# Cached GQA decode block: P·V two steps behind its scores, K three transfers ahead of V, and a last batch that gives o^T by head group

## The chip, the cores and the metric

The kernel runs on one core of a Trainium2 chip. The metric is the device time of one execution in microseconds (us); lower is better. Engines are called as the profile calls them: PE is TensorE (PEld are its weight loads), DVE is VectorE, ACT is ScalarE, POOL is GpSimd and SP is SyncE, which here issues nearly all DMAs. Sixteen DMA engines move the data of all DMAs of the core.

## The reference

A block of grouped-query attention with a cached K and V: 32 batches of 4 query rows each, 32 query heads, 4 K/V heads (a group of 8 query heads shares one), 2048 cached positions, head width 128, everything in bf16.

```python
B, Sq, D = 32, 4, 1024
Hq, Hkv, Sk, Dh = 32, 4, 2048, 128
q = (x @ wq).reshape(B, Sq, Hq, Dh).transpose(0, 2, 1, 3)
k = jnp.repeat(k_cache, rep, axis=1)          # k_cache, v_cache: [B, Hkv, Sk, Dh]
v = jnp.repeat(v_cache, rep, axis=1)
scores = jnp.einsum("bhqd,bhkd->bhqk", q, k) * (Dh ** -0.5)
p = softmax(scores, axis=-1)
o = jnp.einsum("bhqk,bhkd->bhqd", p, v)
return o.transpose(0, 2, 1, 3).reshape(B, Sq, Hq * Dh) @ wo
```

K and V of one batch are 2 MB each, so 128 MB of the cache have to be read once, and wq and wo are 8 MB each.

## The kernel before, in words

Every operation is put on the list of its engine by `p.op` or `p.dma` (lines 26 and 33), with the names of the operations that it waits for. Each engine runs its list strictly in the order written; a wait is a semaphore wait ahead of the instruction. So the order of the Python code is the order on each engine, and what is queued behind a waiting instruction waits too.

**Start.** x and wq are loaded, `Q^T` of all batches is made (line 176) and copied to `QT_sb` (lines 187, 189).

**One batch, called a step.** The loop at line 320 runs over the 32 batches. 128 rows of the score tile are 4 K/V groups by 32 (8 heads by 4 queries). Step i does, in this order on PE:

- `pe_qk(i)`, line 240: 16 matmuls give the scores of batch i in `ps_s`, 128x2048, four PSUM banks. `softmax_max` on DVE reads them (line 280), `softmax_exp` on ACT makes `P_sb` (line 285), `softmax_rinv` on DVE the reciprocal of the row sums (line 290).
- `pe_ot(i-2)`, line 271: one transpose of `o_sb` of batch i-2; ACT copies it to `oT_sb` (line 275). After each eighth batch `oproj` (line 296) multiplies the eight batches by wo: 128 matmuls.
- `pe_fill(i+1, f)` for f = 0 to 7, line 207: K of the *next* batch is transposed, eight 128x128 tiles per fill, and copied to `KT_sb` by DVE (f = 2, 3, 5, 7, line 217) or ACT (line 219).
- `pe_pv(i-1)`, line 248: 64 matmuls P·V of the batch one step behind; ACT scales the result by the reciprocal into `o_sb` (line 265).
- `pe_pt(i, f)` for f = 0, 1, line 225: P of batch i is transposed, and DVE copies it to `PT_sb` (line 231). There is one `PT_sb`, so that copy waits for `pe_pv(i-1)`.

All small PSUM tiles come from a ring of four banks (`slot`, line 194): a new tile waits until the tile four before it has been copied out.

**Loads.** SP issues K and V transfers of 2 MB. `K_sb` and `V_sb` have three buffers each. K of batch b waits for the last fill of batch b-3; V of batch b waits for `pe_pv(b-3)`. The order of the loads is written out: K0, K1, then for each b K(b+2), V(b); wo comes in four parts after V2 to V5. The last V, batch 31, comes in four parts of 512 KB, one for each group, each with its own semaphore.

```python
152        load_k(0)
153        load_k(1)
154        for b in range(B):
155            if b + 2 < B:
156                load_k(b + 2)
157            load_v(b)
158            if b in (2, 3, 4, 5):
159                load_wo(b - 2)
```

**End.** After the loop, from line 346: o^T of batch 30; then P·V of batch 31 for groups 0 to 2 and then for group 3 (lines 351 to 356); ACT scales 96 rows and then 32 rows (lines 357, 359); PE transposes them (363, 371) and DVE copies them to `oT_sb` (364, 372); 96 matmuls with wo for the first 24 heads (line 368), 32 for the last 8 (line 374), in a part of `ps_s`; DVE copies the result to `y_sb` (line 309) and the last four output DMAs are issued by SP and ACT (line 313).

Of the kernel before, what the change touches and what calls it, by code (L numbers as in the profile page):

```python
# [5 lines left out]
ACT = mybir.ActivationFunctionType  # L6
ALU = mybir.AluOpType
AX = mybir.AxisListType
BF16 = mybir.dt.bfloat16
# [47 lines left out]
def bass_standalone__gqa_block_cached__sampling_kernel(  # L57
# [8 lines left out]
    B, Sq, D = x.shape  # L66
    _, G, Sk, Dh = k_cache.shape
# [8 lines left out]
    TV = T // C  # L76
    KT = D // 128
    NKB = 3
    NVB = 3
# [3 lines left out]
    OG = 8  # L83
    NOG = B // OG
    NC = D // 4
    scale = float(Dh) ** -0.5
# [5 lines left out]
    with ExitStack() as es:  # L92
        def sbuf(name, shape, dtype):
            return es.enter_context(nc.sbuf_tensor(name, shape, dtype))

        w_sb = sbuf("w_sb", [128, KT, Hq * Dh], BF16)
        wo_sb = w_sb[:, :, :].rearrange("p a (c n) -> p (a c) n", n=D)
        K_sb = sbuf("K_sb", [128, NKB, T, Dh], BF16)
        V_sb = sbuf("V_sb", [128, NVB, G, TV, Dh], BF16)
# [1 line left out]
        QT_sb = sbuf("QT_sb", [128, B, Hq, Sq], BF16)  # L101
        oT_sb = sbuf("oT_sb", [128, Hq, NT], BF16)
        P_sb = sbuf("P_sb", [128, Sk], BF16)
        PT_sb = sbuf("PT_sb", [128, TV, 128], BF16)
        x_sb = P_sb[:, 0:D]
        xT_sb = P_sb[:, D:2 * D].rearrange("p (a b) -> p a b", b=128)
        o_sb = sbuf("o_sb", [128, Dh], BF16)
# [15 lines left out]
        p = _Program()  # L123
# [8 lines left out]
        def load_k(b):  # L132
            p.dma("sp", lambda e: e.dma_start(
                K_sb[:, b % NKB, :, :], k_cache[b].rearrange("g (r t) d -> (g r) t d", r=R)),
                [("fill", b - NKB, NFILL - 1)] if b >= NKB else [], ("k", b), f"s_k{b % NKB}")
# [13 lines left out]
                wo_sb[:, 8 * c:8 * c + 8, :], wo[c * 1024:(c + 1) * 1024, :].rearrange("(h p) n -> p h n", p=128)),  # L149
                ["qproj"], ("wo", c), f"s_w{c}")  # L150

        load_k(0)
        load_k(1)
        for b in range(B):
            if b + 2 < B:
                load_k(b + 2)
            load_v(b)
            if b in (2, 3, 4, 5):
                load_wo(b - 2)
# [34 lines left out]
        def slot(free):  # L194
            n = len(freed)
            freed.append(free)
            return ring[n % NRING], [freed[n - NRING]]
# [13 lines left out]
        def evac(b, f):  # L211
            buf = slot_of["kt", b, f]
            waits = [("fill", b, f)] + ([("qk", b - 1)] if b else [])
            dst = KT_sb[:, f * TB // C:(f + 1) * TB // C, :, :].rearrange("p v g (r c) -> p (v g) r c", c=C)
            src = buf.rearrange("p (c m r) -> p m r c", c=C, r=R)
            if f in DVE_FILLS:
                p.op("dve", lambda e: e.tensor_copy(dst, src), waits, ("kt", b, f))  # L217
            else:
                p.op("act", lambda e: e.activation(dst, src, ACT.Copy), waits, ("kt", b, f))  # L219

        def pe_pt(i, f):
            buf, waits = slot(("pt", i, f))
            buf = slot_of["pt", i, f] = buf.bitcast(BF16)
            for q in range(8):
                p.op("pe", lambda e, q=q: e.transpose(  # L225
                    buf[:, q * 128:(q + 1) * 128], P_sb[:, (8 * f + q) * 128:(8 * f + q + 1) * 128], ident[:, :]),
                    waits + [("exp", i)] if q == 0 else [], ("ptf", i, f) if q == 7 else None)

        def evac_pt(i, f):
            buf = slot_of["pt", i, f]  # L230
            p.op("dve", lambda e: e.tensor_copy(PT_sb[:, 8 * f:8 * f + 8, :].rearrange("p t q -> p (t q)"), buf),  # L231
                 [("ptf", i, f)] + ([("pv", i - 1)] if i else []), ("pt", i, f))


        def pe_qk(i):
# [11 lines left out]
        def pv_mm(buf, i, g, t, waits, done):  # L247
            p.op("pe", lambda e: e.matmul(  # L248
                buf[32 * g:32 * (g + 1), 0:Dh],
                lhsT=PT_sb[:, t, 32 * g:32 * (g + 1)],  # L250
                rhs=V_sb[:, i % NVB, g, t, :],
                start=(t == 0), stop=(t == TV - 1), tile_position=(0, 32 * g)), waits, done)

        def pe_pv(i):
            buf, waits = slot(("o", i))
            slot_of["o", i] = buf
            waits = waits + [("pt", i, 0), ("pt", i, 1), ("v", i)]
            for t in range(TV):
                for g in range(G):
                    pv_mm(buf, i, g, t, waits if t == 0 and g == 0 else [],  # L260
                          ("pv", i) if (t, g) == (TV - 1, G - 1) else None)

        def o_evac(i):
            buf = slot_of["o", i]
            p.op("act", lambda e: e.activation(o_sb[:, :], buf[:, 0:Dh], ACT.Copy, scale=rinv[:, i:i + 1]),  # L265
                 [("pv", i), ("rinv", i)] + ([("oT", i - 1)] if i else []), ("o", i))

        def pe_ot(i):
            buf, waits = slot(("ot", i))
            buf = slot_of["ot", i] = buf.bitcast(BF16)  # L270
            p.op("pe", lambda e: e.transpose(buf[:, 0:128], o_sb[:, :], ident[:, :]), waits + [("o", i)], ("oT", i))  # L271

        def ot_evac(i):
            buf = slot_of["ot", i]
            p.op("act", lambda e: e.activation(  # L275
                oT_sb[:, :, i * Sq:(i + 1) * Sq], buf[:, 0:128].rearrange("p (h s) -> p h s", s=Sq), ACT.Copy),
                [("oT", i)], ("ot", i))
# [15 lines left out]
        def oproj_mm(buf, n, heads, waits, done):  # L293
            for h in heads:
                for j in range(4):
                    p.op("pe", lambda e, h=h, j=j: e.matmul(  # L296
                        buf[32 * j:32 * (j + 1), 0:NC],
                        lhsT=oT_sb[:, h, 32 * n:32 * (n + 1)],
                        rhs=wo_sb[:, h, NC * j:NC * (j + 1)],
                        start=(h == 0), stop=(h == Hq - 1), tile_position=(0, 32 * j)),  # L300
                        waits if (h, j) == (heads[0], 0) else [], done if (h, j) == (heads[-1], 3) else None)
# [15 lines left out]
        for f in range(NFILL):  # L317
            pe_fill(0, f)
            evac(0, f)
        for i in range(B):  # L320
            pe_qk(i)
            softmax_max(i)
            if i >= 2:
                pe_ot(i - 2)
                ot_evac(i - 2)
                if i % OG == 1 and i > 1:
                    oproj(i // OG - 1)
            if i + 1 < B:
                for f in (0, 1):
                    pe_fill(i + 1, f)  # L330
                    evac(i + 1, f)
            softmax_exp(i)
            if i + 1 < B:
                for f in range(2, NFILL):
                    pe_fill(i + 1, f)
                    evac(i + 1, f)
            softmax_rinv(i)
            if i >= 1:
                pe_pv(i - 1)
                o_evac(i - 1)  # L340
            for f in range(2):
                pe_pt(i, f)
                evac_pt(i, f)


        L = B - 1
        pe_ot(L - 1)
        ot_evac(L - 1)
        o_l, waits = slot(None)
        waits = waits + [("pt", L, 0), ("pt", L, 1)]  # L350
        for t in range(TV):
            for g in range(3):
                pv_mm(o_l, L, g, t, waits + [("v", L, k) for k in range(3)] if t == 0 and g == 0 else [],
                      ("pva", L) if (t, g) == (TV - 1, 2) else None)
        for t in range(TV):
            pv_mm(o_l, L, 3, t, [("v", L, 3)] if t == 0 else [], ("pv", L) if t == TV - 1 else None)
        p.op("act", lambda e: e.activation(o_sb[0:96, :], o_l[0:96, 0:Dh], ACT.Copy, scale=rinv[0:96, L:L + 1]),
             [("pva", L), ("rinv", L), ("oT", L - 1)], "oa")
        p.op("act", lambda e: e.activation(o_sb[96:128, :], o_l[96:128, 0:Dh], ACT.Copy, scale=rinv[96:128, L:L + 1]),
             [("pv", L)], "ob")  # L360
        ta, waits = slot(None)
        ta = ta.bitcast(BF16)
        p.op("pe", lambda e: e.transpose(ta[:, 0:96], o_sb[0:96, :], ident[0:96, 0:96]), waits + ["oa"], "oTa")
        p.op("dve", lambda e: e.tensor_copy(
            oT_sb[:, 0:24, L * Sq:(L + 1) * Sq], ta[:, 0:96].rearrange("p (h s) -> p h s", s=Sq)), ["oTa"], "ota")
        y_l = ps_s[:, 0:512]
        n = NOG - 1
        oproj_mm(y_l, n, range(24), ["ota", ("ot", L - 1)], None)
        tb, waits = slot(None)
        tb = tb.bitcast(BF16)  # L370
        p.op("pe", lambda e: e.transpose(tb[:, 0:32], o_sb[96:128, :], ident[96:128, 96:128]), waits + ["ob"], "oTb")
        p.op("dve", lambda e: e.tensor_copy(
            oT_sb[:, 24:32, L * Sq:(L + 1) * Sq], tb[:, 0:32].rearrange("p (h s) -> p h s", s=Sq)), ["oTb"], "otb")
        oproj_mm(y_l, n, range(24, 32), ["otb"], ("op", n))
        oproj_evac(y_l, n)
        for m in range(NOG - 1):
            oproj_out(m, ("sp",))
# [57 lines left out]
```

## Time and profile before

| | us |
|---|---|
| device time, median of 8 runs (lowest, highest) | 386.81 (384.85, 387.41) |
| the profiled execution's own device time | 384.93 |
| its span in the profile | 383.1 |
| mean busy share of DMA engines in most of its 40 slices | 0.9 or more |
| DVE / PE / ACT busy | 273.9 / 281.0 / 208.5 |
| first 2 MB K transfer issued after the first batch's fills | 34.17 |
| last wait of the fills for K (batch 31) ends | 358.43 |

The eight runs were 384.93, 384.85, 387.41, 387.25, 386.56, 387.06, 386.49 and 387.32 us. The profile covers one execution. Its span is 1.8 us shorter than that execution's device time. Busy times are sums over the span; where an engine idles, the profile names the event that ended the idle time.

### The profile page before, as it was taken

To read this page: it belongs to the slowest core of one execution; us is meant where nothing else is said; L and a number is where in the kernel's file an instruction comes from. 1 tells how busy PE (TensorE), PEld (TensorE's weight loads), DVE (VectorE), ACT (ScalarE), POOL (GpSimd) and SP (SyncE) were. 2 spreads that over 40 slices of the span, in tenths; PEclk is the share of its full clock that TensorE was granted. 3 is DMA by queue.
4 is the path that set the end of the run, shared out by engine and by line. 5 is a ranking of instruction groups with operands and counts; after the bars stand their busy time and mean duration, and the time that the engine had idled before them with its cause. 6 is when DMAs were issued, how large, how long until landed. Compare 5 with 4: busy or idle time off the path is not lost.

```text
span 383.1 us, 12595 instructions
## 1 busy us (share of the span) xinstructions
PE 281.0 (73%) x5929; PEld 230.6 (60%) x5929; DVE 273.9 (71%) x299; ACT 208.5 (54%) x261; POOL 0.7 (0%) x6
## 2 busy tenths in 40 slices
PE   1976788575483877888777678877758877887756
PEld 1965666465382757666655567665547666665545
DVE  0017999682643883999888848998887858996960
ACT  1006777364261655677666627765656647765640
POOL 0000000000000000000000000000000000000000
PEclk9999999986867998999999999999998999998999
DMA  8999999999999999999999999999999999999950
GB/s 328 433 431 418 417 414 398 414 408 400 412 403 416 414 423 411 415 418 417 417 421 414 415 419 414 414 417 417 416 420 417 414 423 414 419 418 409 403 204 9
DMA packets 27251, 152.32 MB, mean 398 GB/s; under 512 B 1472, under 2 KB 1984, under 8 KB 22592
## 3 DMA queue, kind: packets, MB, share of 16 engines
q1 hardware_dynamic: 27104, 151.49, 96.7%
q8 instruction: 46, 0.75, 0.8%
q10 hardware_dynamic: 96, 0.03, 0.0%
q14 instruction: 5, 0.04, 0.0%
HBM read 151.26 MB, written 0.26 MB: 395 GB/s over the span
## 4 chain that ended last, share of the span: by engine, by line
DMA 58%; PE 17%; ACT 12%; DVE 9%; issue 2%; SPq 0%
DMA K_sb<-in_k_cache_dram 52%; ACT KT_sb L219 6%; DMA w_sb<-in_wq_dram 6%; ACT P_sb L285 6%; PE ps_r L207 4%; DVE KT_sb L217 4%; DVE mx L280 4%; PE ps_r L296 3%; PE ps_r L248 3%; PE ps_s L240 2%; PE ps_r L225 2%; PE ps_s L296 1%; DVE PT_sb L231 1%; PE ps_s L176 1%; DVE QT_sb L187 0%
## 5 line engine op out<-in xcount | busy, mean ns | idle before, releaser
L207 PE MATMUL ps_r<-ident,K_sb 128*128 128x128 bf16 x2048 | 144.8, 232 | 65.5 <-DMA K_sb<-in_k_cache_dram 38.2
L217 DVE COPY KT_sb<-ps_r 128x1024 bf16<-128x1024 bf16 x128 | 148.0, 1217 | 41.7 <-PE ps_r L207 41.4
L207 PEld LDWEIGHTS ps_r<-ident,K_sb 128*128 128x128 bf16 x2048 | 128.3, 105 | 80.9 <-DMA K_sb<-in_k_cache_dram 40.4
L219 ACT ACTIVATE KT_sb<-ps_r 128x1024 bf16<-128x1024 bf16 x128 | 124.4, 1025 | 73.1 <-PE ps_r L207 73.1
L280 DVE TENSOR_REDUCE mx<-ps_s 128x1 f32<-128x2048 f32 x32 | 73.3, 2292 | 6.4 <-PE ps_s L240 4.0
L285 ACT ACTIVATE P_sb<-ps_s,negmx 128x2048 bf16<-128x2048 f32 x32 | 63.0, 1969 | 2.2 <-DVE negmx L281 2.1
L231 DVE COPY PT_sb<-ps_r 128x1024 bf16<-128x1024 bf16 x64 | 41.3, 686 | 14.2 <-PE ps_r L225 12.3
L248 PE MATMUL ps_r<-V_sb,PT_sb 128*32 128x128 bf16 x2048 | 35.4, 220 | 15.6 <-ACT KT_sb L219 10.8
L248 PEld LDWEIGHTS ps_r<-V_sb,PT_sb 128*32 128x32 bf16 x2048 | 29.7, 97 | 21.0 <-ACT KT_sb L219 17.0
L275 ACT ACTIVATE oT_sb<-ps_r 128x128 bf16<-128x128 bf16 x31 | 8.6, 277 | 54.4 <-PE ps_r L271 54.4
L240 PE MATMUL ps_s<-KT_sb,QT_sb 128*32 128x512 bf16 x512 | 33.9, 382 | 2.4 <-DVE KT_sb L217 1.7
L225 PE MATMUL ps_r<-ident,P_sb 128*128 128x128 bf16 x512 | 34.3, 220 | 1.4 <-ACT P_sb L285 1.2
L225 PEld LDWEIGHTS ps_r<-ident,P_sb 128*128 128x128 bf16 x512 | 28.7, 98 | 5.0 <-ACT P_sb L285 1.4
L240 PEld LDWEIGHTS ps_s<-KT_sb,QT_sb 128*32 128x32 bf16 x512 | 10.8, 95 | 13.2 <-issue 2.5
L187 DVE CAST QT_sb<-ps_r 128x512 bf16<-128x512 f32 x2 | 1.3, 686 | 22.3 <-PE ps_r L176 22.3
L265 ACT ACTIVATE o_sb<-ps_r,rinv 128x128 bf16<-128x128 f32 x31 | 11.4, 367 | 9.0 <-PE ps_r L248 9.0
L189 ACT ACTIVATE QT_sb<-ps_r 128x512 bf16<-128x512 f32 x2 | 1.1, 594 | 25.9 <-PE ps_r L176 25.9
L176 PE MATMUL ps_s<-P_sb,w_sb 128*128 128x128 bf16 x128 | 10.0, 241 | 6.6 <-DMA w_sb<-in_wq_dram 6.5
L296 PE MATMUL ps_r<-w_sb,oT_sb 128*32 128x256 bf16 x384 | 11.5, 273 | 3.5 <-issue 2.3
L176 PEld LDWEIGHTS ps_s<-P_sb,w_sb 128*128 128x128 bf16 x128 | 8.9, 109 | 7.1 <-issue 4.4
L296 PEld LDWEIGHTS ps_r<-w_sb,oT_sb 128*32 128x32 bf16 x384 | 10.0, 97 | 4.6 <-issue 3.4
L271 PEld LDWEIGHTS ps_r<-ident,o_sb 128*128 128x128 bf16 x31 | 3.0, 96 | 12.7 <-issue 12.7
(30 smaller groups left out, 58.7 us busy)
## 6 DMA issues: line engine op xcount, KB each, us to landing
K_sb<-in_k_cache_dram SPq DMA_DIRECT2D x32, 2048.0 KB, 25.0
V_sb<-in_v_cache_dram SPq DMA_DIRECT2D x31, 2048.0 KB, 27.1
w_sb<-in_wq_dram SPq DMA_DIRECT2D x4, 2048.0 KB, 14.2
w_sb<-in_wo_dram SPq DMA_DIRECT2D x4, 2048.0 KB, 24.5
V_sb<-in_v_cache_dram SPq DMA_DIRECT2D x4, 512.0 KB, 15.4
P_sb<-in_x_dram SPq DMA_DIRECT2D x1, 256.0 KB, 2.8
out_dram<-y_sb SPq DMA_DIRECT2D x14, 16.0 KB, 11.6
out_dram<-y_sb ACTq DMA_DIRECT2D x2, 16.0 KB, 1.6
```

What stands on the lines that cost most here:

```text
L176: p.op("pe", lambda e, kt=kt, h=h: e.matmul(ps_q(h), lhsT=w_sb[:, kt, h * Dh:(h + 1) * Dh], rhs=xT_sb[:, kt, :], start=(kt == 0 and h % 4 ...
L207: p.op("pe", lambda e, q=q, t=t: e.transpose(buf[:, q * 128:(q + 1) * 128], K_sb[:, b % NKB, t, :], ident[:, :]), waits + [("k", b), "iden ...
L217: p.op("dve", lambda e: e.tensor_copy(dst, src), waits, ("kt", b, f))
L219: p.op("act", lambda e: e.activation(dst, src, ACT.Copy), waits, ("kt", b, f))
L225: p.op("pe", lambda e, q=q: e.transpose(buf[:, q * 128:(q + 1) * 128], P_sb[:, (8 * f + q) * 128:(8 * f + q + 1) * 128], ident[:, :]), wai ...
L231: p.op("dve", lambda e: e.tensor_copy(PT_sb[:, 8 * f:8 * f + 8, :].rearrange("p t q -> p (t q)"), buf), [("ptf", i, f)] + ([("pv", i - 1)] ...
L240: p.op("pe", lambda e, c=c, g=g: e.matmul(ps_s[32 * g:32 * (g + 1), c * 512:(c + 1) * 512], lhsT=QT_sb[:, i, REP * g:REP * (g + 1), :], rh ...
L248: p.op("pe", lambda e: e.matmul(buf[32 * g:32 * (g + 1), 0:Dh], lhsT=PT_sb[:, t, 32 * g:32 * (g + 1)], rhs=V_sb[:, i % NVB, g, t, :], star ...
L265: p.op("act", lambda e: e.activation(o_sb[:, :], buf[:, 0:Dh], ACT.Copy, scale=rinv[:, i:i + 1]), [("pv", i), ("rinv", i)] + ([("oT", i - ...
L280: p.op("dve", lambda e: e.tensor_reduce(mx[:, i:i + 1], ps_s[:, :], AX.X, ALU.max), [("qk", i)], ("mx", i))
L285: p.op("act", lambda e: e.activation(P_sb[:, :], ps_s[:, :], ACT.Exp, bias=negmx[:, i:i + 1], scale=scale, accum_out=ssum[:, i:i + 1]), [( ...
L296: p.op("pe", lambda e, h=h, j=j: e.matmul(buf[32 * j:32 * (j + 1), 0:NC], lhsT=oT_sb[:, h, 32 * n:32 * (n + 1)], rhs=wo_sb[:, h, NC * j:NC ...
```

## The change

Four edits are made together.

1. K is loaded three transfers ahead: K0, K1, K2, then for each b K(b+3), V(b).
2. P·V runs two steps behind: step i does `pe_pv(i-2)` and `pe_ot(i-3)`, and `oproj` of a block of eight batches comes one step later. `PT_sb` gets two buffers, and the copy into it waits for `pe_pv(i-2)`.
3. In the last step, 12 matmuls 128x128 by 128x512 on `ident` and a part of wo are put on PE after `pe_pv(29)`; their output is not used. DVE multiplies `P_sb` of batch 31 by the reciprocals, and the transposes of P wait for that.
4. The end: P·V of batch 30 comes after the loop. P·V of batch 31 is computed with V as the stationary operand, for each group g by itself: 16 matmuls of 128x128 by 128x32 give o^T of the group directly, DVE copies it to `oT_sb`, and 32 matmuls with wo follow for its 8 heads. The order on PE is P·V 0, P·V 1, transpose of o(30), wo 0, P·V 2, wo 1, P·V 3, wo 2, wo 3.

```diff
-        PT_sb = sbuf("PT_sb", [128, TV, 128], BF16)
+        PT_sb = sbuf("PT_sb", [128, 2, TV, 128], BF16)
...
-        load_k(0)
-        load_k(1)
+        for b in range(NKB):
+            load_k(b)
         for b in range(B):
-            if b + 2 < B:
-                load_k(b + 2)
+            if b + NKB < B:
+                load_k(b + NKB)
             load_v(b)
...
         def evac_pt(i, f):
             buf = slot_of["pt", i, f]
-            p.op("dve", lambda e: e.tensor_copy(PT_sb[:, 8 * f:8 * f + 8, :].rearrange("p t q -> p (t q)"), buf),
-                 [("ptf", i, f)] + ([("pv", i - 1)] if i else []), ("pt", i, f))
+            p.op("dve", lambda e: e.tensor_copy(PT_sb[:, i % 2, 8 * f:8 * f + 8, :].rearrange("p t q -> p (t q)"), buf),
+                 [("ptf", i, f)] + ([("pv", i - 2)] if i > 1 else []), ("pt", i, f))
...
+        def pe_idle(n):
+
+            buf, waits = slot("idle")
+            for k in range(n):
+                p.op("pe", lambda e: e.matmul(buf, lhsT=ident[:, :], rhs=wo_sb[:, 0, 0:512], start=True, stop=True),
+                     waits + [("wo", 0)] if k == 0 else [], "idle" if k == n - 1 else None)
+
+        L = B - 1
         for i in range(B):
             pe_qk(i)
             softmax_max(i)
-            if i >= 2:
-                pe_ot(i - 2)
-                ot_evac(i - 2)
-                if i % OG == 1 and i > 1:
+            if i >= 3:
+                pe_ot(i - 3)
+                ot_evac(i - 3)
+                if i > OG and i % OG == 2:
                     oproj(i // OG - 1)
...
-            if i >= 1:
-                pe_pv(i - 1)
-                o_evac(i - 1)
+            if i >= 2:
+                pe_pv(i - 2)
+                o_evac(i - 2)
+            if i == L:
+                pe_idle(12)
+                p.op("dve", lambda e: e.tensor_scalar(P_sb[:, :], P_sb[:, :], rinv[:, L:L + 1], None, op0=ALU.mult),
+                     [("rinv", L)], ("pn", L))
             for f in range(2):
-                pe_pt(i, f)
+                pe_pt(i, f, ("pn", L) if i == L else ("exp", i))
                 evac_pt(i, f)
...
+        pe_ot(L - 2)
+        ot_evac(L - 2)
+        pe_pv(L - 1)
+        o_evac(L - 1)
+        y_l = ps_s[:, 0:512]
+        n = NOG - 1
+
+        def pv_last(g):
+            buf, waits = slot(("otl", g))
+            for t in range(TV):
+                p.op("pe", lambda e, t=t: e.matmul(
+                    buf[:, 0:32], lhsT=V_sb[:, L % NVB, g, t, :], rhs=PT_sb[:, L % 2, t, 32 * g:32 * (g + 1)],
+                    start=(t == 0), stop=(t == TV - 1)),
+                    waits + [("v", L, g), ("pt", L, 0), ("pt", L, 1)] if t == 0 else [],
+                    ("pvl", g) if t == TV - 1 else None)
+            p.op("dve", lambda e: e.tensor_copy(
+                oT_sb[:, 8 * g:8 * (g + 1), L * Sq:(L + 1) * Sq], buf[:, 0:32].rearrange("p (h s) -> p h s", s=Sq)),
+                [("pvl", g)], ("otl", g))
+
+        def oproj_last(g):
+            oproj_mm(y_l, n, range(8 * g, 8 * (g + 1)), [("otl", g), ("ot", L - 1), ("exp", L)],
+                     ("op", n) if g == G - 1 else None)
+
+        pv_last(0)
+        pv_last(1)
         pe_ot(L - 1)
         ot_evac(L - 1)
...
+        oproj_last(0)
+        pv_last(2)
+        oproj_last(1)
+        pv_last(3)
+        oproj_last(2)
+        oproj_last(3)
         oproj_evac(y_l, n)
```

The lines of the old end (351 to 374) are taken out.

## The prediction

> **What bounds the kernel now.** I read the page's 40 slices first, then the chain that ended last, then the end of it in stretches of 1 us, then the timeline of the last 30 us. From the page:
>
> ```profile
> DMA  8999999999999999999999999999999999999950
> ...
> q1 hardware_dynamic: 27104, 151.49, 96.7%
> ...
> DMA 58%; PE 17%; ACT 12%; DVE 9%; issue 2%; SPq 0%
> ```
>
> The reader is to see that the DMA engines never rest between the first and the 38th slice: the stream of 151 MB sets the time, and what a change can win is a hole in the stream, or the tail after it. The 39th slice is half busy, and the stretches show why:
>
> ```profile
> 363.00:364.00 1.00, 0.07 (x5) 0.06 (x8) 1.00 (x2) 1.00 (x2) 0.00 (x0) 1.00 1.02 395
> 364.00:365.00 1.00, 1.00 (x65) 0.90 (x66) 0.67 (x2) 0.80 (x1) 0.00 (x0) 1.00 0.77 293
> ...
> 370.00:371.00 1.00, 0.35 (x11) 0.17 (x11) 0.00 (x0) 1.00 (x1) 0.00 (x0) 1.00 0.50 205
> ...
> 373.00:374.00 1.00, 0.33 (x18) 0.33 (x21) 0.62 (x2) 0.11 (x1) 0.00 (x0) 1.00 0.19 48
> 374.00:375.00 1.00, 1.00 (x54) 1.00 (x46) 0.00 (x0) 0.20 (x1) 0.00 (x0) 1.00 0.00 0
> ```
>
> (The last two columns are DMA share and GB/s.) From 364 to 373.4 half of the sixteen engines work alone at 205 GB/s: half ran ahead by some 9 us, and a transfer has landed when the slow half has brought its part. The stream ends at 373.4. Now the chain's end:
>
> ```profile
> 333.95 24.43 DMA K_sb<-in_k_cache_dram
> 358.38 0.05 issue
> ...
> 369.56 2.07 ACT P_sb L285 x2
> 371.63 0.05 issue
> 371.67 0.63 PE ps_r L225 x8
> 372.31 0.02 issue
> 372.33 1.30 DVE PT_sb L231 x2
> 373.63 0.04 issue
> 373.68 1.76 PE ps_r L248 x64
> ```
>
> K31 lands at 358.38 and 15.3 us of compute follow until P^T of batch 31 is ready at 373.63. That is 0.2 us after the end of the stream. So two paths meet at 373.6: the engines' from K31, and the DMA's to V31's last part. After it P·V, scaling, transpose, wo, copy and output take 383.1 - 373.6 = 9.5 us, with the DMAs at rest. That is where the change works.
>
> [...] after 6.27 us of waiting for K the stretch 90 to 95 us has a granted clock of 0.50; waits of 2 us near the end leave it at 1.00. [...]
>
> **The loads, edit 1.** The bytes are the same, so the stream's end moves only if it gets a hole. Per step the waits are alike: K(b) to be filled, then V, one step older in K's favour. When K(b) lands in the steady state, the transfers already issued behind it are V(b-2), K(b+1), V(b-1), K(b+2), V(b) before, and V(b-3), K(b+1), V(b-2), K(b+2), V(b-1) after: five of 2 MB each way, 25 us of stream at 415 GB/s, against a 9 us lead of the fast half. Two places differ.
> (a) The front. V0 now stands on SP behind K3, which waits for fill 7 of batch 0; SP issues K3 at 34.17 in the trace, and that fill depends on wq and K0 alone. Issued by then are x, wq and three K: 0.26 + 8.39 + 6.29 = 14.9 MB; the 2 us stretches sum to 13.7 MB moved at 34.0. The rest, 1.2 MB at 425 GB/s, lasts to 36.9. A 16 KB output DMA takes 1.6 us from issue to landing, so K3's data starts by 35.8. No hole, with about 1 us to spare; the cost is between 0 and 0.5 us, and I take 0. At 42.42 (K4's issue) 19.1 MB are issued and 17.2 moved, and the gap widens from there.
> (b) The end. After K31 come V28, V29, V30 and V31, instead of three V. On the slow half a transfer takes 5.05 us (K30 ended its wait at 348.34, K31 at 358.43, 10.1 for two), so K31 lands at about 353.4, 5.05 earlier. V31 waits for P·V of batch 28, in step 30, behind the fills of batch 31. Before, P·V ended 6.6 us after K31 landed (365.0 less 358.4): now 359.9, when V28 (358.4) is there. The slow half needs V31's parts at 368.3; 8 us of margin. The fast half would want them at 359.4 and idles some 2 us, out of its 9 us lead: no cost.
>
> **Two steps behind, edit 2.** Per step PE, DVE and ACT get the same instructions in the same order, only with older data; the ring has the same 12 tiles per step. What is new is K's lead: the engines must be 5.05 us earlier. An unhindered step takes 8.65 us (scores at 318.83 and 327.47), which is what DVE's own sum gives: 2.29 + 0.15 + 4.62 + 0.15 + 1.29 = 8.5, against 10.1 of DMA. A step with `oproj` took 14.3 (304.49 to 318.83), and the last one moves from step 25 to 26. From K26 at about 302: scores 26 at 309.5, 27 at 323.8, then 332.5, 341.1; the fills of K30 would start 1.0 later at 342.1, while K30 lands at 343.3. So K31 is waited for again by a little over a microsecond, and its 353.4 holds. Cost 0; cover 1.2 us.
>
> **The last step, edit 3.** From 353.4 as in the trace from 358.4: scores 31 end 361.9, max 364.25, exp with its accumulator read 366.6, reciprocal 366.8. New on DVE: the scaling of P, [...] gives 367.5. The 12 matmuls of 512 columns on PE: line 240's 512 columns take 1.05 us for 16, four side by side, that is 0.25 each less start-up; 12 x 0.22 = 2.6. They follow P·V 29 (V29 lands at 363.5, done 364.6) and end at 367.2, so they fit into the wait for exp. Then two transposes of 8 and two copies, 1.9 as in 371.67 to 373.6: P^T of batch 31 ready at 369.4, which was 373.63. P·V 30 waits for V30, 368.5, and ends at 369.7. Both are ahead of V31's second part. [...]
>
> **The new end, edit 4.**
>
> ```profile
> 355.39 3.77 SPq L145 DMA_DIRECT2D V_sb<-in_v_cache_dram  x4
> ...
> 375.88 2.81 PE L296 MATMUL ps_s<-w_sb,oT_sb 128*32 128x256 bf16 x96 [0.30 <-DVE oT_sb L364]
> ...
> 380.18 0.42 DVE L309 CAST y_sb<-ps_s 128x256 bf16<-128x256 f32 x1 [1.16 <-PE ps_s L296]
> ```
>
> V31's parts take 14.4 to 15.6 us to land from starts of 355.4 to 357.9; with the end at 373.4 and a quarter of 5 us each they land at about 369.8, 371.0, 372.2 and 373.4, before and after alike.
> Removed behind 373.6: P·V 1.76, ACT 0.36, transpose and copy 0.6, transpose and copy 0.5, about 3.2 net of overlaps with 4.2 us of wo matmuls (2.81 + 1.06 and gaps).
> Added: 64 matmuls with 128-wide weights and 32 moving columns. No row shows that shape. Above: the transposes of line 225, 128 columns, 1.07 for 16, near 58 ns each, 0.93 per group. [...] I take 40 ns, 0.65. A group of wo matmuls is 32 x 27 ns (96 in 2.81 less 0.2 of start-up) = 0.87.
> In PE's order: P·V 1 starts with its V at 371.0, ends 371.7; transpose of o(30) 0.23 and ACT's copy 0.28, 372.3 with signals; wo 0 373.2; P·V 2 373.8; wo 1 374.7; P·V 3 375.35 (its V long there); wo 2 376.2, in which DVE's copy of group 3 (0.17) is hidden; wo 3 377.1, drained 377.3; copy 0.42, 377.7; output 383.1 - 380.6 = 2.5: span 380.2. That is 2.9 less. At 58 ns it is 1.1 worse (four groups)[...]. PE also loses time to "issue" that nothing in the view explains: 2.29 at 147.9, 1.67 at 227.8, 1.35 at 309.7, and 0.7 at 369.4, within waiting. In the tail PE has no slack now; between 0 and 1.5, I take 0.4. Sum -2.5 us: span 380.6, device time 384.93 - 2.5 = 382.4. The profiled run is one of the two fast ones of eight; against the median of 386.81 the forecast is 384.3.
>
> **Rivals.**
> 1. The forecast, 384.3: the tail loses 1.2 to 4 us. Chance 0.64.
> 2. The tail's gain is eaten: 58 ns per matmul (-1.1), [...] or an issue stall of 1.5 take 2 to 2.5 away. For it: PE is now serial from 371 to 377, in nine pieces. Against: each would have to come at its bad end, two of three together. Time 386.5. Chance 0.2.
> 3. Slower: the engines cannot follow K's lead. Place: steps 26 to 31, after the late `oproj`. For it: DVE is 8.5 of 10.1 us busy per step, and the lead asks for 5 us. Against: the 1.2 us of K wait worked out above. It decides once the engines are later than K31 by the slack of 1.2 and the gap between P^T and P·V 30 (0.3), that is 1.5, plus the 2.5 of gain and 1.2 of resolution: 5.2 us of lateness, for instance a half clock in the last steps plus two stalls of 2 us. With 8 us, V31 begins to be issued late too: 386.8 + 8 - 4 = 390.8. Chance 0.11.
> 4. The change doesn't reach the end: the stream gets a hole of 2 to 2.5 us at the front, (a) having started later than worked out. 386.8. Chance 0.05.
>
> **How the numbers follow.** 0.3% (1.16 us) is about what can be told from no change. Faster (below 385.65): rival 1, and a little of rival 2: 0.66. Same: 0.2, from rivals 2 and 4 and the forecast's edge. Slower: 0.14, rival 3 and the tails of 2 and 4. The range: [...] the upper end takes in rivals 2 and 4, 386.8.
>
> **What would show it.** Right: DMA share near 1 until 364 with the stream's end within 0.5 us of 373.4, K31's wait ending near 353, P^T of batch 31 ready before V31's second part, and a tail of about 7 us behind the stream. Wrong: a dip in the share at 35 to 37 us; no wait for K30 and K31 at the end; more than 0.93 us for a group of the new P·V; a granted clock below 1.00 in the last 15 us.

## The result, and the profile after

All edits together: median 383.29 us (383.10 to 384.62, 11 runs) beside 386.48 us (384.85 to 387.41, 32 runs) of the kernel before. The ratio is 0.9925, 95% interval 0.991 to 0.9939, which is 2.9 us less (the medians lie 3.2 us apart). The profiled execution took 383.13 us, with a span of 381.3 us: only 1.8 us under the 383.1 us of the profiled execution before. The larger part of what follows is about the 1.1 us between these two differences.

From the page of the kernel after, the clock and the DMA engines in 40 slices:

```profile
PEclk9999999997669699999999999999999999999999
DMA  8999999999999999999999999999999999999971
```

The stream has no hole at the front that it did not have before (its share is 0.84 from 36 to 37 us, and 0.83 in the kernel before), and its end lies where it was. In stretches of 1 us (last three columns: granted clock, DMA share, GB/s):

```profile
358.00:359.00 1.00, 0.20 (x16) 0.20 (x20) 1.00 (x2) 1.00 (x2) 0.00 (x0) 1.00 1.01 397
359.00:360.00 1.00, 1.00 (x68) 0.90 (x57) 0.53 (x2) 0.73 (x2) 0.00 (x0) 1.00 0.66 254
360.00:361.00 1.00, 1.00 (x20) 0.82 (x21) 0.53 (x1) 0.30 (x1) 0.00 (x0) 1.00 0.59 238
361.00:362.00 1.00, 1.00 (x17) 0.31 (x9) 0.85 (x3) 0.00 (x0) 0.00 (x0) 1.00 0.89 332
362.00:363.00 1.00, 0.02 (x1) 0.00 (x0) 1.00 (x1) 0.28 (x1) 0.00 (x0) 1.00 1.00 410
...
373.00:374.00 1.00, 1.00 (x40) 0.76 (x31) 0.00 (x0) 0.00 (x0) 0.00 (x0) 1.00 0.24 66
374.00:375.00 1.00, 0.32 (x7) 0.03 (x7) 0.19 (x1) 0.00 (x0) 0.00 (x0) 1.00 0.01 2
```

The share falls to 0.59 and is back at 1.00 from 362 on. Read as the prediction reads a share of 0.50, the fast half of the DMA engines runs dry after 359 and waits some 2 us for V31, which is issued at 359.92 behind P·V 28. The rest goes on, and the stream ends in the same stretch as before, 373 to 374 (66 GB/s there, then 2). Now the last step and the end, from the timeline:

```profile
353.29 2.41 PE L207 MATMUL ps_r<-ident,K_sb 128*128 128x128 bf16 x40 [1.31 <-DMA K_sb<-in_k_cache_dram]
...
366.71 0.75 DVE L351 TENSOR_SCALAR P_sb<-P_sb,rinv 128x2048 bf16<-128x2048 bf16 x1
...
368.18 1.29 DVE L231 COPY PT_sb<-ps_r 128x1024 bf16<-128x1024 bf16 x2 [0.72 <-PE ps_r L225]
...
371.35 0.56 PE L368 MATMUL ps_r<-PT_sb,V_sb 128*128 128x32 bf16 x16 [0.67 <-DMA V_sb<-in_v_cache_dram]
...
373.92 0.40 PE L296 MATMUL ps_s<-w_sb,oT_sb 128*32 128x256 bf16 x7
...
375.02 0.94 PE L296 MATMUL ps_s<-w_sb,oT_sb 128*32 128x256 bf16 x25 [0.70 <-issue]
...
376.39 1.93 PE L296 MATMUL ps_s<-w_sb,oT_sb 128*32 128x256 bf16 x64
```

K31 lands 5.1 us earlier than before (353.29 for 358.43), P^T of batch 31 is ready at 369.47 for 373.63, and PE waits for V31's second part at 371.35 with P^T long there. The two paths that met at 373.6 are apart. From the stream's end at about 373.4 it is 7.9 us to the end of the span, where it was 9.7. In the middle of wo 1 stands a gap that the program has no wait for: seven matmuls, 0.70 us of "issue" (time in which the engine waits for nothing that the profile shows), 25 matmuls.

### The profile page after: what moved, and what is told of

Its sections match the earlier page's. It is cut to its first block, busy times and chain, and to the rows that moved or that the text cites. A ratio compares the mean times of both kernels' runs of the same rounds, so it can differ in the third digit from the quotient of the medians.

```text
span 381.3 us, 12614 instructions
## 1 busy us (share of the span) xinstructions
PE 278.6 (73%) x5938; PEld 225.1 (59%) x5939; DVE 274.9 (72%) x302; ACT 207.2 (54%) x259; POOL 0.7 (0%) x6
## 4 chain that ended last, share of the span: by engine, by line
DMA 59%; PE 17%; ACT 11%; DVE 9%; issue 3%; SPq 1%
DMA K_sb<-in_k_cache_dram 56%; ACT KT_sb L219 6%; PE ps_r L207 6%; DVE KT_sb L217 5%; ACT P_sb L285 5%; PE ps_r L296 3%; DMA V_sb<-in_v_cache_dram 3%; PE ps_r L248 3%; DVE mx L280 2%; PE ps_s L240 2%; PE ps_r L225 2%; PE ps_s L296 1%; DVE PT_sb L231 1%; SPq L129 0%; PE ps_r L368 0%
## 5 line engine op out<-in xcount | busy, mean ns | idle before, releaser
L207 PE MATMUL ps_r<-ident,K_sb 128*128 128x128 bf16 x2048 | 139.2, 226 | 63.1 <-DMA K_sb<-in_k_cache_dram 36.4
L207 PEld LDWEIGHTS ps_r<-ident,K_sb 128*128 128x128 bf16 x2048 | 122.1, 101 | 79.8 <-DMA K_sb<-in_k_cache_dram 37.2
L248 PE MATMUL ps_r<-V_sb,PT_sb 128*32 128x128 bf16 x1984 | 33.4, 220 | 15.8 <-ACT KT_sb L219 12.8
L248 PEld LDWEIGHTS ps_r<-V_sb,PT_sb 128*32 128x32 bf16 x1984 | 28.0, 97 | 20.9 <-ACT KT_sb L219 18.5
L240 PE MATMUL ps_s<-KT_sb,QT_sb 128*32 128x512 bf16 x512 | 34.7, 385 | 4.0 <-DVE KT_sb L217 1.7
```

Of the source, the lines that this page charges most:

```text
L207: p.op("pe", lambda e, q=q, t=t: e.transpose(buf[:, q * 128:(q + 1) * 128], K_sb[:, b % NKB, t, :], ident[:, :]), waits + [("k", b), "iden ...
L240: p.op("pe", lambda e, c=c, g=g: e.matmul(ps_s[32 * g:32 * (g + 1), c * 512:(c + 1) * 512], lhsT=QT_sb[:, i, REP * g:REP * (g + 1), :], rh ...
L248: p.op("pe", lambda e: e.matmul(buf[32 * g:32 * (g + 1), 0:Dh], lhsT=PT_sb[:, i % 2, t, 32 * g:32 * (g + 1)], rhs=V_sb[:, i % NVB, g, t, : ...
```

## The experiments

The ratio of each is to runs of the kernel before beside it. The median of those runs moves between 386.21 and 387.15 us from set to set, so ratios of different sets differ where the times do not: all edits (383.29, 0.9925) and e7 (383.32, 0.9904) are equal.

| run | what it is | median us (range) | ratio, 95% interval |
|---|---|---|---|
| e1 | edits 1 and 2, old end | 385.60 (384.73 to 386.74) | 0.997 [0.996, 0.998] |
| e2 | edits 3 and 4, old order | 386.22 (385.98 to 387.92) | 0.9996 [0.9986, 1.0005] |
| e3 | all, without the 12 matmuls | 383.06 (382.61 to 383.21) | 0.9903 [0.9886, 0.992] |
| e4 | all, transpose of o(30) early | 383.14 (383.08 to 383.35) | 0.9908 [0.9891, 0.9925] |
| e5 | before, one more profile | 386.96 | one run |
| e6 | e1 with the 12 matmuls | 385.25 (384.19 to 385.48) | 0.9948 [0.9932, 0.9964] |
| e7 | all, P not scaled | 383.32 (382.96 to 383.42) | 0.9904 [0.9891, 0.9917] |
| e8 | e4 without the 12 matmuls | 383.13 (382.82 to 383.21) | 0.9898 [0.9886, 0.9911] |
| e9 | e4, 60 narrow matmuls for the 12 | 382.91 (382.28 to 384.04) | 0.9903 [0.9881, 0.9925] |
| e10 | before, with 10 matmuls in its waits | 385.03 (384.84 to 385.30) | 0.9961 [0.9945, 0.9976] |
| e11 | all edits again | 383.50 (383.25 to 383.65) | 0.9917 [0.99, 0.9934] |
| e12 | e9, 5 of the matmuls later | 382.78 (382.20 to 383.02) | 0.989 [0.9872, 0.9908] |

### Which half brings the gain: e1 and e2

e1 keeps the old end behind the loop (with `PT_sb[:, i % 2, ...]`) and drops the 12 matmuls and the scaling:

```diff
-            if i == L:
-                pe_idle(12)
-                p.op("dve", lambda e: e.tensor_scalar(P_sb[:, :], P_sb[:, :], rinv[:, L:L + 1], None, op0=ALU.mult),
-                     [("rinv", L)], ("pn", L))
             for f in range(2):
-                pe_pt(i, f, ("pn", L) if i == L else ("exp", i))
+                pe_pt(i, f, ("exp", i))
```

> Edits 1 and 2 alone: K three transfers ahead, P*V two steps behind, two P^T buffers; the old end is kept (scale on ACT, two transposes). Theory (the two paths, K31 to P^T and stream to V31, met at 373.6, so that either half alone wins little): the stream still ends at 373.4; the engines' path gets 4 to 5 us of slack, P^T of batch 31 is ready near 369; the old end follows V31 as before, only that groups 0 to 2 can start when their parts have landed (372.5), which lets about 0.9 us of it overlap. Span about 382.2, against 383.1 of the profiled run before, ratio near 0.997. Rival A (the lead is the whole gain): ratio near 0.9925, as with all edits. Rival B (the new end is the whole gain): ratio 1.000.

e2 is the kernel before with these lines in the last step and the new end:

```diff
+            if i == L:
+                pe_idle(12)
+                p.op("dve", lambda e: e.tensor_scalar(P_sb[:, :], P_sb[:, :], rinv[:, L:L + 1], None, op0=ALU.mult),
+                     [("rinv", L)], ("pn", L))
             for f in range(2):
-                pe_pt(i, f)
+                pe_pt(i, f, ("pn", L) if i == L else ("exp", i))
```

> Edits 3 and 4 alone: the old order of loads and P*V one step behind; in the last step the 12 matmuls and the scaling of P, then o^T by head group. Theory: P^T of batch 31 is then the later path, 0.75 us later than before because of the scaling on DVE (about 374.4), and nothing of the new end overlaps the stream: four groups of 0.5 + 0.87 us in a row, copy and output end at about 383: ratio between 0.997 and 1.001. Rival B (the new end is the whole gain): ratio near 0.9925. Rival A: 1.000 or a little above.

e1 wins 0.3%, e2 nothing that can be told from 0, all edits 0.75%. Neither rival holds: each half takes work from a path while the other path still ends at 373.6, and both are needed. In e2 the chain shows both the 12 matmuls (370.64 to 373.18, longer than the wait that should hold them) and the copies of P^T (to 374.96) ahead of the new end.

The expected ratio of e1 was met, but not its span: 384.9 where 382.2 was worked out. The timeline of its profiled execution shows why:

```profile
366.72 1.86 PE L225 MATMUL ps_r<-ident,P_sb 128*128 128x128 bf16 x16 [2.03 <-ACT P_sb L285]
...
372.94 3.16 PE L248 MATMUL ps_r<-V_sb,PT_sb 128*32 128x128 bf16 x64 [1.47 <-DMA V_sb<-in_v_cache_dram]
```

The transposes took 1.86 us where the kernel before took 1.07, and the last P·V 3.16 where it took 1.76. The granted clock was 0.50 from 366 to 378. At 386.70 this is the second longest of e1's 19 executions, 1.1 us above their median of 385.60, so it can't stand for all of them.

### The clock in the tail: e5, e6, e10

That raised a question on the kernel before itself. Its runs lie in groups, near 385, 386.2 and 387.2 (some 6, 12 and 14 of the 32 runs), and the profile that the prediction was worked from belongs to the first. e5 is a second profiled execution of it.

> The kernel before, unchanged, for another profiled execution: its runs lie in groups near 385, 386.2 and 387.2 us, and the execution profiled so far (384.93) is one of the quickest. Theory (a half clock in the tail makes the groups): an execution near 386 or 387 us has the stream's end at 373.4 as before, and a granted clock of 0.5 in part of the last 18 us, as in the run with edits 1 and 2 alone, where it was 0.50 from 366 to 378. Rival (the loads vary): the clock is 1.00 there and the stream ends 1 to 2 us later.

It took 386.96. The stretch 372 to 378, first of the profiled execution before:

```profile
372.00:378.00 6.00, 4.82 (x160) 4.38 (x161) 1.50 (x3) 1.00 (x3) 0.00 (x0) 1.00 0.10 32
```

and of e5, with two rows of its timeline in a second fence:

```profile
372.00:378.00 6.00, 5.02 (x84) 4.38 (x85) 1.59 (x3) 1.00 (x3) 0.00 (x0) 0.50 0.09 28
```

```profile
371.53 1.89 PE L225 MATMUL ps_r<-ident,P_sb 128*128 128x128 bf16 x16 [1.23 <-ACT P_sb L285]
...
374.20 3.16 PE L248 MATMUL ps_r<-V_sb,PT_sb 128*32 128x128 bf16 x64 [0.68 <-DVE PT_sb L231]
```

PE does 84 matmuls in these 6 us and not 160, at a clock of 0.50 and not 1.00. The stream ended in the same stretch in both (47 and 48 GB/s in 373 to 374). Up to 369 the two executions are within 0.2 us of each other; of the 2.1 us between their spans 1.9 come with transposes and P·V at half clock: P·V starts 0.5 us later and takes 1.4 us longer. e10 tests this as a cause, by giving PE work in its waits:

```diff
+            if i == B - 1:
+                pe_idle(5, "idle0")
             if i >= 1:
                 pe_pv(i - 1)
                 o_evac(i - 1)
+            if i == B - 1:
+                pe_idle(5, "idle1")
```

> The kernel before with 5 matmuls of 512 columns ahead of P*V 30 and 5 behind it, in the last step, where PE waits for V30 and for exp; outputs not used. Theory (the slower groups of the kernel before, 386 and 387, are executions in which the clock falls to 0.5 in the tail): the clock stays at 1.00 to the end, all runs lie near 385.0, ratio about 0.996. Rival (the groups have another cause): the same spread as before, ratio 1.000.

All seven runs lie between 384.84 and 385.30, beside 11 runs of the kernel before from 384.85 to 387.47; its profile has a clock of 1.00 to the end and P·V 31 at 1.76 us again:

```profile
373.58 1.76 PE L248 MATMUL ps_r<-V_sb,PT_sb 128*32 128x128 bf16 x64 [0.93 <-PE ps_r L271]
```

```profile
374.00:376.00 2.00, 1.70 (x61) 1.47 (x56) 0.21 (x1) 0.72 (x2) 0.00 (x0) 1.00 0.00 0
```

So the spread of the kernel before is a matter of a warm or a cold tail (a clock of 1.00 or of 0.50), and keeping it warm is worth 0.4% by itself (385.03 us, a ratio of 0.9961). (An execution of the group near 386.2 was not profiled; that it is a shorter stretch at half clock is likely, not shown.) With the tail warm in both, all edits bring 383.3 to 383.5 against 385.0, a gain of 1.5 to 1.7 us, near the 1.8 us of the two profiles.

e6 puts the 12 matmuls into e1.

```diff
+            if i == L:
+                pe_idle(12)
             for f in range(2):
```

> Edits 1 and 2 with the old end, and the 12 matmuls of edit 3 ahead of the transposes of P in the last step (no scaling). Theory (half clock in the tail cost the run with edits 1 and 2 alone its gain): the clock is 1.00 when the last P*V starts, the wo matmuls take 27 ns each, span about 382.2, time 384.0, ratio near 0.994. Rival (the 12 matmuls do nothing here, as they did nothing beside the new end): the same as with edits 1 and 2 alone, ratio 0.997.

Half as expected: the ratio went from 0.997 to 0.9948, but the medians are only 0.35 us apart (385.60 and 385.25; the kernel before was slower beside e6, 387.15 for 386.52). In the profiled execution (385.36) PE waited 2.07 us for V31 ahead of the last P·V, the clock fell to 0.50 at 373.2, and P·V took 3.01 us. Twelve matmuls at 364.6 did not keep the clock up through the wait from 370.5 to 372.6. Two of the six runs (384.19, 384.56) are near the 384.0 expected with a warm tail.

This changes how e1 and e2 are to be read. The profiled execution of e2 (386.27) has a clock of 1.00 to the end, as the quick executions of the kernel before have, and it is 1.0 to 1.4 us slower than e10's runs. With the clock taken out, the new end in the old order loses about a microsecond, the lead alone gains under one (by those two runs of e6, which were not profiled), and together they gain 1.5 to 1.7.

### What edit 3 does beside the new end: e3, e7

e3 leaves out the call of `pe_idle(12)`.

> All edits, but without the 12 matmuls whose output is not used. Theory: PE then has a gap of 2.8 us (364.7 to 367.5) ahead of the transposes of P, shorter than the gaps of 4 to 7 us after which the granted clock fell to 0.5; the clock stays at 1.00 in the last 15 us and the time is that of all edits within 0.3 us. Rival (the matmuls carry the clock): the granted clock shows 0.5 somewhere between 367 and 375 and the time is 1.5 to 3 us longer than with all edits.

The time is that of all edits or a little less, but not for the reason given. A gap of 2.98 us did bring the clock to 0.50, from 366.6 to 373.4, and P·V 30 took 1.90 us for 1.08:

```profile
367.63 1.89 PE L225 MATMUL ps_r<-ident,P_sb 128*128 128x128 bf16 x16 [2.98 <-DVE P_sb L350]
```

PE gave away its waits for V31 and still came to wo 1 0.73 us later (374.65 for 373.92). There it lost next to nothing in the gap that holds PE up with all edits, so that P·V 3 followed at 375.98 for 375.89, and by then the clock was back at 1.00. In four runs no cold end was seen; whether one can come without the 12 matmuls stays open.

e7 takes out the scaling of P, that is the `tensor_scalar` and the wait for it; the rows of the last batch are left unnormalised.

> All edits without the scaling of P of the last batch on DVE: the last batch's rows are left unnormalised. Theory (the scaling is hidden, as P^T of batch 31 stands ready before the first part of V31 has landed): the time with all edits, within 0.3 us, ratio 0.991 to 0.993. Rival (the 0.75 us of DVE is on the path): 0.75 us less than with all edits.

383.32 beside 383.29 and 383.50 with it: hidden, as the prediction had it. P·V 0 of batch 31 starts at 370.11 for 370.13, behind V31's first part in both.

### The gap in wo 1: e4, e8, e9, e12

e4 has wo 0 ahead of P·V 1, so that both waits of PE at 371 and 372 hold work.

```diff
         pv_last(0)
-        pv_last(1)
         pe_ot(L - 1)
         ot_evac(L - 1)
         oproj_last(0)
+        pv_last(1)
```

> All edits, with the order on PE at the end changed: P*V 0, transpose of o(30), wo 0, P*V 1, P*V 2, wo 1, P*V 3, wo 2, wo 3. Theory: PE is serial from V31's second part on and waits 0.67 us for it and 0.46 us for the copy of o(30); with the transpose and wo 0 ahead of P*V 1, both waits hold work: about 1 us less than with all edits (ratio to the kernel before near 0.990). Rival (the end is set by the last part of V31 landing at 373.5, or by instruction stalls of PE): the same time as with all edits, ratio 0.9925.

Its median is 0.15 and 0.36 us under the two of all edits (383.29, and 383.50 in e11), where 1 us was expected. PE came to the eighth matmul of wo 1 earlier, at 373.87, and stood there until 375.05; in the order of all edits it stood there until 375.02, in e11 until 375.54. Without the 12 matmuls (e3) it stood, for a shorter time, at the twentieth. The place moves with the number of instructions ahead of it. In the kernel before a like gap lies within P·V 30, behind 53 of its 64 matmuls; in e10, with five more ahead of it, behind 48. First the kernel before, then e10:

```profile
370.12 0.35 PE L248 MATMUL ps_r<-V_sb,PT_sb 128*32 128x128 bf16 x11 [0.54 <-issue]
```

```profile
370.02 0.41 PE L248 MATMUL ps_r<-V_sb,PT_sb 128*32 128x128 bf16 x16 [0.56 <-issue]
```

e8 is e4 without the 12 matmuls.

> All edits with the transpose of o(30) and wo 0 ahead of P*V 1, and without the 12 matmuls. The early transpose alone won nothing: PE then stood 1.18 us at one instruction in wo 1 (the eighth matmul), until 375.05, where it had stood 0.70 us until 375.02 in the old order; without the 12 matmuls PE stood 0.08 us at the twentieth. Theory (PE's own instructions come in blocks, and the one that begins there arrives at about 375.0, after the stream): without the 12 the block begins 12 matmuls later, PE reaches it nearer to 375.0, and the end comes 0.3 us earlier than with either edit alone, 382.8 us. Rival (the half clock without the 12 costs something once the waits are filled): 383.3 or more.

Inconclusive by its time (383.13), as PE stood at the twentieth matmul until 375.37, not 375.0. e9 moves the place by 48 pairs of weight load and matmul:

```diff
-                pe_idle(12)
+                pe_idle(60)
...
-                p.op("pe", lambda e: e.matmul(buf, lhsT=ident[:, :], rhs=wo_sb[:, 0, 0:512], start=True, stop=True),
+                p.op("pe", lambda e: e.matmul(buf[:, 0:96], lhsT=ident[:, :], rhs=wo_sb[:, 0, 0:96], start=True, stop=True),
```

> All edits with the early transpose, and 60 matmuls of 96 columns in place of the 12 of 512 (about as long: 60 x 43 ns = 2.6 us, but 48 instruction pairs more). Theory (PE's instructions come in blocks of a fixed count, 16 KB each by the size of the instruction DMAs, 0.75 MB in 46 packets, that is 128 pairs of weight load and matmul[...]): the place where PE stands moves 48 pairs earlier, from the eighth matmul of wo 1 to the twenty-fourth of wo 0; PE stands there until about 372.7 and not until 375.0, and the end comes 0.5 to 1 us earlier than with all edits: about 382.4. Rival (the wait is for something that belongs to wo 1, its operand or its slot): PE stands at the eighth matmul of wo 1 again and the time is 383.1 to 383.3.

PE in e9, from the timeline:

```profile
370.97 0.84 PE L296 MATMUL ps_s<-w_sb,oT_sb 128*32 128x256 bf16 x23 [0.46 <-ACT oT_sb L275]
372.81 0.50 PE L296 MATMUL ps_s<-w_sb,oT_sb 128*32 128x256 bf16 x9 [1.00 <-issue]
...
374.21 1.90 PE L296 MATMUL ps_s<-w_sb,oT_sb 128*32 128x256 bf16 x32
```

Behind the twenty-third matmul of wo 0, until 372.81, and no gap in wo 1: the place is as expected, and the rival, a wait that belongs to wo 1, falls. The moment up to which PE stands there is near the 372.7 expected, which was an estimate of the author's. The end did not come at 382.4: wo 1 took 1.90 us for 1.06, at half clock (0.50 in 374 to 376), and half of its runs are at 383.3 or above. e12 puts five wide matmuls into the wait ahead of wo 0:

```diff
-                pe_idle(60)
+                pe_idle(55, 96, "idle")
...
         ot_evac(L - 1)
+        pe_idle(5, 512, "idle2")
         oproj_last(0)
```

> As the run with 60 narrow matmuls, but 55 of 96 columns ahead of the transposes of P and 5 of 512 columns between the transpose of o(30) and wo 0, where PE waited 0.46 us for ACT's copy. That run's times lay near 382.4 and near 383.3, and in its profiled execution (383.31) the clock was 0.50 from 374 to 376. Theory (the two groups are a warm and a cold tail; up to its twenty-fourth matmul wo 0 has about 1 us to give away, because PE stands there until 372.8 anyhow): the clock stays at 1.00 and all runs lie near 382.4, ratio near 0.9895. Rival (the groups have another cause, or the 5 matmuls of 0.22 us push the end out): 383.3 or more in half of the runs, as there.

From its timeline, and the clock in a stretch:

```profile
373.22 0.50 PE L296 MATMUL ps_s<-w_sb,oT_sb 128*32 128x256 bf16 x9 [0.97 <-issue]
...
374.55 1.06 PE L296 MATMUL ps_s<-w_sb,oT_sb 128*32 128x256 bf16 x32
```

```profile
374.00:376.00 2.00, 2.00 (x73) 1.74 (x69) 0.38 (x2) 0.00 (x0) 0.00 (x0) 1.00 0.04 8
```

Warm to the end with the same gap, so the gap alone does not bring the half clock; and all four runs (382.20 to 383.02) lie under the quickest of the 16 runs of all edits (383.10). The gap still ends late, at 373.22 here, and only one run came under the 382.4. The median is 0.5 to 0.7 us under those of all edits, 0.1 to 0.2%, from sets that did not run side by side, and the intervals of e12 and e11 overlap: more I would not claim for it. e11, all edits once more beside e9 and e10, gave what was expected of it:

> All edits, unchanged, beside the two others on the same chip: 383.3 us, ratio 0.991 to 0.9935.

## Why the prediction was right, and where not

The forecast of 384.3 (-2.5 us) was right in direction and near in size. The path was right. That the size came so near is partly luck: the shorter tail gave 1.8 us and not 2.5, and a gain of about 1.1 us from the clock, which the forecast did not have, made up for it.

**The loads (edit 1).** As predicted. No dip at 35 to 37 us beyond that of the kernel before, so rival 4 fell; K31's wait ended at 353.29 (353.4 worked out), with 1.31 us of waiting ahead of it (1.2). The share fell to 0.59 for some 2 us at no cost: the stream ended in 373 to 374 as before. The parts of V31 came a little later than estimated: the second at 371.3 and not 371.0.

**Two steps behind (edit 2).** The engines followed K's lead, so rival 3 fell. Scores of batch 31 began at 360.81 and ended at 361.86 (361.9). K30 was not waited for, as the step before it came 1 us later than worked out (a gap of 1.08 us at 324.4 that the chain calls "issue"); K31 was.

**The last step (edit 3).** The scaling took 0.75 us and ended at 367.46 (367.5, an estimate of the author's: no row of the profile before shows this operation), P^T stood ready at 369.47 (369.4). What the prediction said of the clock, "waits of 2 us near the end leave it at 1.00", does not hold even in the trace that it was read from: the wait for K30 is 1.84 us long, the clock falls to 0.50 at its end, from 348.24 to 351.66, and 56 transposes of K take 4.86 us, where 40 take 2.41 at 358.43:

```profile
348.35 4.86 PE L207 MATMUL ps_r<-ident,K_sb 128*128 128x128 bf16 x56 [1.84 <-DMA K_sb<-in_k_cache_dram]
```

It fell to 0.50 with the gaps of e6 and e3 too, 2.07 and 2.98 us, and stayed at 1.00 after one of 1.59 us with all edits (363.61). By their times (26 of 32 above 385.8) most executions of the kernel before are likely to have a stretch at 0.50 in the tail; e5 is the one that shows it.

**The new end (edit 4).** The term of 64 matmuls at 40 ns, 0.65 a group, an estimate of the author's, was too dear: 16 took 0.50 (P·V 2, 373.42 to 373.92), 31 ns each. Two groups, P·V 2 and P·V 3, lie on the path, so this gave 0.3 us. The term "issue, 0 to 1.5, I take 0.4" was too cheap: from the start of wo 1 to that of P·V 3 it took 1.97 us (373.92 to 375.89), and from wo 0 to P·V 2 without a gap 0.99, so the gap cost 0.98 us, of which PE's row shows 0.70; in e11 the same reading gives 1.73. Against the 380.6 of the sum that is 0.6 more; wo 0 and wo 1 at 0.99 for 0.87 are 0.2 more, the start of wo 0 at 372.43 for 372.3 and small terms 0.2 more. With the 0.3 less this makes the 381.3 of the span. Rival 2 named this stall, but its matmuls at 58 ns did not come.

**The step that failed** is the carrying over from the profile to the median: "against the median of 386.81 the forecast is 384.3". It took the 1.9 us between this median and the profiled execution (384.93) as a constant that both kernels have. It is a cold tail of 1.2 to 2.1 us (e10 beside its own runs of before, e5 beside the first profile), which the kernel after, by its times, mostly doesn't pay: its runs spread 1.5 us and all but two lie within 0.5. So 1.8 us came from the shorter tail, where 2.5 were forecast, and about 1.1 from the clock, where none were.

Why the kernel after is spared was not isolated. e3 shows that it is not the 12 matmuls alone; the new end has PE busy from 372.4 on but for the gap in wo 1, where the old end had PE wait for ACT, a transpose and a copy between P·V and wo.

## What to carry to other kernels

Where two paths meet at the same moment, shortening either alone wins next to nothing: e1 won 0.3% and e2 nothing, both 0.75% (of which about 0.3% is the clock). Before a difference of a few microseconds is worked out from one profile, ask where that execution lies among the runs, and if they form groups, profile one of another group: the group may be a cost that the change removes. And in a short serial end of many small matmuls, count PE's instructions as well as its time: here PE stood still behind its weight load 5707 or 5834 (or 5835), whatever work came there.

## What was not expected of the hardware

- PE stood for 0.46 to 1.45 us (in e3 for less) at places fixed by the count of its instructions. Counted from the program's start, by the order of the program and the traces' rows, it stood behind 5707 weight loads in the kernel before, e2, e5 and e10, and behind 5834 or 5835 in all edits, e3, e4, e7, e8, e9, e11 and e12, whatever work came there: 127 or 128 pairs of weight load and matmul apart. (In e1 and e6 PE came to the second place only at 376.8 or later, and did not stand.) The page of the kernel before counts 46 packets of instruction DMA, 0.75 MB together, and 5929 pairs; if all packets were PE's, that would be some 129 pairs for a packet. In the last 80 us of the kernel before and of all edits they come 3.8 to 9.7 us apart, and each of the two stops there has one: 367.59 to 368.69 for 370.12 before, 372.35 to 373.34 for 375.02 with all edits, so it began 2.5 and 2.7 us before PE went on and ended 1.4 and 1.7 us before. What PE waits for is not shown. That it is its next block of instructions is the author's reading: the records don't name the engine that a packet is for, and why a packet comes when it does was not tested.
- The clock fell to 0.50 although PE was not idle, and in these traces it changes on a grid of time. In the clock records of the kernel before and of all edits each of the 24 whole stretches between two changes lasts 3.41 us or a multiple of it (up to 249.17). The stretches at 0.50 in the tails of the experiments, read from their windows, agree: 3.4 us in e6 and e9 (both from 373.2) and in e8 (from 368.2), 6.8 in e3 (from 366.6), 6.83 in e5 (from 371.19), 13.65 in e1 (from 365.14). The grid's place against the program's start differs: a change of the first profile is at 348.24, one of e5 at 371.19, 6.7 steps later. What parts a warm tail from a cold one is not shown; PE's busy time alone does not sort the cases. The 3.41 us ahead of the fall in e5, 367.78 to 371.19, hold 1.29 us of PE work, and the step of the grid nearest to it in the first profile, 368.72 to 372.13, holds 1.66, and the clock stays; but in e9 the clock fell behind 3.41 us with 1.85 us of work. In e1 it stayed at 0.50 through P·V 30, a wait of 1.5 us and 3.16 us of P·V 31, up to 378.8.
- A pair of a 128-wide weight load and a matmul of 32 columns took 31 ns in a row of 16 (P·V 2 with all edits, 16 in 0.50 us at a clock of 1.00).
